# A decode kernel whose first two loads are issued ahead of the opening barrier, and whose closing barrier is taken without GpSimd's drain, with GpSimd waiting for the store

## The chip, the cores and the metric

The kernel runs on one core of one Trainium2 chip. The metric is the time of one execution on the device, in microseconds (us), as the timer gives it. A profile has its own length, the span, from the first to the last instruction that it records; for this kernel the timer reads 1.8 us more than the span. All runs whose times are compared were in the same (fast) state. SP, ACT, DVE, PE and GpSimd (POOL in the profile) are the five engines; SP and ACT issue the loads and stores here.

## The reference, cut to what matters

```python
# x (1,1,640); k_cache, v_cache (1,32,32768,128); wq (640,4096); wo (4096,640)
# w_gate, w_up (640,1728); w_down (1728,640); all bfloat16
xn = layernorm(x)
q  = xn @ wq                                       # 32 heads of 128
p  = softmax(q . k_cache * 128**-0.5)              # one query, 32768 keys for each head
attn = (p . v_cache) @ wo
ffn  = (silu(xn @ w_gate) * (xn @ w_up)) @ w_down
out  = x + attn + ffn                              # 640 numbers
```

Each of the 32 heads has its own K and its own V of 8 MiB. They are read once and used once, so the job is to read 554 MB.

Of the kernel before, what the change touches and what calls it, by code (L numbers as in the profile page):

```python
# [12 lines left out]
def bass_parallel_sum__gqa_block_cached__swiglu_ffn__decode_kernel(  # L13
# [18 lines left out]
    NCD = D // 128  # L32
# [46 lines left out]
    with ExitStack() as es:  # L79
# [3 lines left out]
        def sem(name):  # L83
            return es.enter_context(nc.semaphore(name))
# [32 lines left out]
        s_x, s_wq, s_out = sem("x"), sem("wq"), sem("o")  # L117
# [13 lines left out]
        s_att, s_fin = sem("att"), sem("fin")  # L131
        s_xr, s_or = sem("xr"), sem("orow")
        s_ob, s_op, s_ot = sem("o_blocks"), sem("o_ps"), sem("o_rows")
        block = es.enter_context(nc.Block())

        flat = ring[:, :, :].rearrange("p s n -> p (s n)")
        wq = flat[:, WQ_S * CE:WQ_S * CE + NCD * H * DH]
        x0 = WQ_S * CE + NCD * H * DH
        xrow = flat[0:1, x0 + NCD * 128:x0 + NCD * 128 + D]
        xrow_v = xrow.rearrange("o (m c) -> o m c", c=NCD)  # L140
        xnb = flat[:, x0:x0 + NCD * 128].rearrange("p (c m) -> p c m", c=NCD)
        assert NCD * (H * DH + 256) <= CE
        wq_v = wq.rearrange("p (c n) -> p c n", c=NCD)
        f0 = FFN_S * CE
        wg = flat[:, f0:f0 + NCD * F]
        wu = flat[:, f0 + NCD * F:f0 + 2 * NCD * F]
# [15 lines left out]
        def kv_src(cache, h, j0, n):  # L162
            return cache[0, h].rearrange("(p j) d -> p (j d)", p=128)[:, j0 * DH:(j0 + n) * DH]

        def counter(e, h0):

            group = [None]

            def wait(sem_of, h, count):
                n = count(h)  # L170
                if group[0] is not None:
                    d = count(h + PER) - n
                    assert n >= 1 and all(count(h + PER * i) == n + d * i for i in range((H - h0) // PER))
                    n = group[0] * d + n
                e.wait_ge(sem_of, n)

            return group, wait

        def at(tile, h, n, i):

            start = h * n if i is None else i * (PER * n) + h * n
            return tile[:, bass.ds(start, n)]

        with nc.psum_tensor("ps8", [128, 8, 512], F32) as ps8:
# [10 lines left out]
            @block.sync  # L195
            def sp(e):
                owner = {}
                for u in units:
                    s = slot_of[u]
                    if s in owner:  # L200
                        e.wait_ge(*owner.pop(s))
                    if u[0] == "wq":
                        e.dma_start(wq, A_wq.rearrange("(p c) n -> p (c n)", c=NCD)).then_inc(s_wq, 16)  # L203
                        owner[s] = (s_q, NQB)
                    elif u[0] == "k":
                        e.dma_start(ring[:, s, :], kv_src(A_k_cache, u[1], 0, NJ)).then_inc(s_slot[s], 16)
                        owner[s] = (s_qk, NHF * (u[1] + 1))
                    elif u == LASTV:
                        j = 0
                        for i, n in enumerate(TAIL):  # L210
                            e.dma_start(ring[:, s, j * DH:(j + n) * DH],
                                        kv_src(A_v_cache, u[1], j, n)).then_inc(s_tail[i], 16)
                            j += n
                    elif u[0] == "v":
                        e.dma_start(ring[:, s, :], kv_src(A_v_cache, u[1], 0, NJ)).then_inc(s_slot[s], 16)
                        owner[s] = (s_pv, u[1] + 1)
                    elif u[0] == "ffn":
                        e.dma_start(wg, B_w_gate.rearrange("(p c) n -> p (c n)", c=NCD)).then_inc(s_ffn[0], 16)
                        e.dma_start(wu, B_w_up.rearrange("(p c) n -> p (c n)", c=NCD)).then_inc(s_ffn[1], 16)
                        e.dma_start(flat[:, d0:d0 + FM * D], B_w_down[0:FM * 128, :].rearrange(  # L220
                            "(p j) n -> p (j n)", j=FM)).then_inc(s_ffn[2], 16)
                        e.dma_start(wd[0:FL, FM, :], B_w_down[FM * 128:F, :]).then_inc(s_ffn[2], 16)
                    else:
                        wo_src = A_wo.rearrange("(p j) n -> p (j n)", j=OC)
                        j = 0
                        for i, n in enumerate(WTAIL):
                            e.dma_start(wo[:, j * D:(j + n) * D], wo_src[:, j * D:(j + n) * D]).then_inc(s_wo[i], 16)  # L227
                            j += n
                e.wait_ge(s_fin, 2)
                e.dma_start(out[0, 0:1, :].rearrange("o (c m) -> (o c) m", c=NCD), orow[:, :]).then_inc(s_out, 16)  # L230
                e.wait_ge(s_out, 16)

            @block.gpsimd
            def pool(g):
                n = [0]

                def done(ins):
                    ins.then_inc(s_const, 1)
                    n[0] += 1
                    g.wait_ge(s_const, n[0])  # L240

                for t in (ident, identf):
                    done(g.memset(t[:, :], 0.0))
                    done(g.affine_select(out=t[:, :], in_=t[:, :], compare_op=ALU.not_equal, fill=1.0, base=0,
                                         pattern=[[-1, 128]], channel_multiplier=1))
                done(g.memset(blk[:, :], 0.0))
                for a in range(RB):
                    done(g.tensor_copy(out=fold32[a * 32:(a + 1) * 32, :],
                                       in_=ident[a * 32:(a + 1) * 32, a * 32:a * 32 + OC]))
                for a in range(RB):  # L250
                    done(g.memset(blk[a * 32:(a + 1) * 32, a:a + 1], 1.0))
                assert n[0] == 5 + 2 * RB

            @block.tensor
            def pe(t):
# [172 lines left out]

            @block.scalar
            def act(a):  # L430
                a.dma_start(xrow, A_x[0, 0:1, :]).then_inc(s_x, 16)
                a.sem_inc(s_ov, 1)
                a.wait_ge(s_a, 8)
                a.activation(out=st[:, 4:5], in_=st[:, 3:4], func=ACTF.Sqrt).then_inc(s_aa, 1)
                for b in range(NQB):
                    a.wait_ge(s_q, b + 1)
                    a.activation(out=qb[:, b * 512:(b + 1) * 512], in_=bank[b], func=ACTF.Copy).then_inc(s_qc, 1)

                group, wait = counter(a, HA)

                def evac(h):
                    wait(s_pv, h, lambda h: h + 1)
                    wait(s_rz, h, lambda h: h + 1)
                    if h >= 1 and group[0] is None:
                        a.wait_ge(s_fold, h)
                    a.activation(out=o4[:, :], in_=O, func=ACTF.Copy,  # L446
                                 scale=rzb[0:W, h % SR:h % SR + 1]).then_inc(s_o4, 1)

                def column(h):
                    wait(s_fold, h, lambda h: h + 1)  # L450
                    a.activation(out=at(ocol, h, 1, group[0]), in_=fold_ps, func=ACTF.Copy).then_inc(s_ov, 1)  # L451

                def softmax(h):
                    wait(s_neg, h, lambda h: h + 1)
                    a.activation(out=P[:, h % PR, :], in_=sc[:, :], func=ACTF.Exp,  # L455
                                 bias=negb[:, h % SR:h % SR + 1], scale=c_scale,
                                 accum_out=rsum[:, h % SR:h % SR + 1]).then_inc(s_exp, 1)

                def step(h):
                    if h >= 3:  # L460
                        column(h - 3)
                    if h >= 2:
                        evac(h - 2)
                    softmax(h)

                for h in range(HA):
                    step(h)
                with a.Fori(0, (H - HA) // PER) as i:
                    group[0] = i
                    for h in range(HA, HA + PER):  # L470
                        step(h)
                    group[0] = None
                column(H - 3)
                evac(H - 2)
                column(H - 2)
                a.wait_ge(s_op, 1)
                a.activation(out=ot[:, :], in_=op, func=ACTF.Copy).then_inc(s_ot, 1)
                a.wait_ge(s_f, 1)
                a.activation(out=sg[:, 0, 0:FB - 1], in_=ffn[:, 0:FB - 1], func=ACTF.Exp,
                             scale=-1.0).then_inc(s_fa, 1)  # L480
                a.activation(out=sg[0:FL, 0, FB - 1:FB], in_=ffn[0:FL, FB - 1:FB], func=ACTF.Exp,
                             scale=-1.0).then_inc(s_fa, 1)
# [140 lines left out]
```

## The kernel before: the parts that the change and the argument touch

All large loads go through a ring of three slots in SBUF, and SP issues all of them in order: wq, K0, K1, V0, K2, V1, ... until the last V, the three FFN weights and wo. Before it reuses a slot, SP waits until its last user has read it. ACT issues the one small load, of x (1280 bytes). Each engine's program is a branch of one block; a block ends with a barrier of all engines. The framework puts another barrier in front of it, after GpSimd has set a few constants.

```python
        s_ob, s_op, s_ot = sem("o_blocks"), sem("o_ps"), sem("o_rows")
        block = es.enter_context(nc.Block())       # default closing barrier
        # ... (cut)

            @block.sync
            def sp(e):
                owner = {}
                for u in units:                    # wq, K0, K1, V0, K2, V1, ...
                    s = slot_of[u]
                    if s in owner:
                        e.wait_ge(*owner.pop(s))
                    if u[0] == "wq":
                        e.dma_start(wq, A_wq.rearrange("(p c) n -> p (c n)", c=NCD)).then_inc(s_wq, 16)
                        owner[s] = (s_q, NQB)
                    elif u[0] == "k":
                        e.dma_start(ring[:, s, :], kv_src(A_k_cache, u[1], 0, NJ)).then_inc(s_slot[s], 16)
                        # ... (cut: V, FFN weights, wo)
                e.wait_ge(s_fin, 2)
                e.dma_start(out[0, 0:1, :].rearrange("o (c m) -> (o c) m", c=NCD), orow[:, :]).then_inc(s_out, 16)
                e.wait_ge(s_out, 16)               # the store has landed

            @block.gpsimd
            def pool(g):
                n = [0]

                def done(ins):                     # each constant waits for the one before
                    ins.then_inc(s_const, 1)
                    n[0] += 1
                    g.wait_ge(s_const, n[0])
                # ... (cut: identity matrices and masks)
                for a in range(RB):
                    done(g.memset(blk[a * 32:(a + 1) * 32, a:a + 1], 1.0))
                assert n[0] == 5 + 2 * RB

            @block.scalar
            def act(a):
                a.dma_start(xrow, A_x[0, 0:1, :]).then_inc(s_x, 16)
                # ... (cut)
```

## Time and profile before

| | before |
|---|---|
| time, median of 4 runs (lowest to highest) | 1288.67 us (1288.64 to 1289.19) |
| span of the profile | 1286.8 us |
| moved, rate over the span | 554 MB, 431 GB/s |
| PE, DVE busy | 81%, 52% |
| first packet of wq moves at | 1.79 us |
| issue of the store to the end of the span | 1.58 us |

The page of the kernel before, cut to its DMA lines. The rows DMA and GB/s have one entry for each fortieth of the span; a 9 is 90% or more of the 16 DMA engines busy.

```profile
DMA  9999999999999999999999999999999999999998
GB/s 422 426 424 449 426 430 441 430 434 428 440 428 432 444 428 432 440 430 434 428 440 428 432 444 428 432 440 428 434 428 442 428 432 444 428 432 440 428 418 358
...
q1 hardware_dynamic: 11178, 554.00, 99.7%
```

The loads bound this kernel. They are never starved: the queue of SP was busy for 99.7% of the time of all 16 engines, and only the first and the last of the 40 slices contain a stretch without load. PE and DVE idle for a part of every head, waiting for K or V. The Trainium skill, "DMA: Bandwidth & Descriptors", section "Specifications", gives 435 GB/s as the ceiling of the fabric, and the 431 GB/s of this trace agrees with that.

The timeline of the kernel before, from 0 to 17 us, cut to loads and to what uses them. Columns: start and length in us, engine (SPq and ACTq are the queues that issue), line, operation, written<-read, count, and in brackets how long the engine had been idle and what ended it.

```profile
0.74 0.52 ACTq L431 DMA_DIRECT2D ring<-in_A_x_dram  x1
0.75 0.42 SPq L203 DMA_DIRECT2D ring<-in_A_wq_dram  x1
1.23 0.88 SPq L206 DMA_DIRECT2D ring<-in_A_k_cache_dram  x2
...
2.04 0.35 PE L260 MATMUL ps<-one,ring 1*128 1x1 bf16 x5 [2.04 <-DMA ring<-in_A_x_dram]
...
6.16 0.82 DVE L513 COPY ring<-xn 128x640 bf16<-128x640 bf16 x1
...
16.26 1.01 PE L275 MATMUL ps<-ring 128*128 128x512 bf16 x2 [11.17 <-DMA ring<-in_A_wq_dram]
```

The packets of the same kernel from 0 to 4 us, one entry for each 0.1 us (bytes are counted where a packet starts; the 13 is x, what follows is wq):

```profile
GB/s 0 0 0 0 0 0 0 0 0 0 0 0 0 0 0 0 13 819 1229 3277 410 410 0 0 0 410 0 0 0 0 0 0 0 0 0 0 0 0 0 1229
```

So the layernorm (PE L260 to DVE L513) is done at 6.98 us, and then PE waits until wq lands, for 9.3 us.

The instructions of the opening barrier in the kernel before (the view of one source line, here the framework's). Columns: operation, count, duration in ns (min/median/max), first and last start in us.

```profile
L608 POOLq EVENT_SEMAPHORE  x2: 17/17/17, 0.5 to 0.6; - x2
L608 SPq DRAIN  x1: 7/7/7, 0.0 to 0.0; - x1
...
L608 SPq EVENT_SEMAPHORE  x1: 17/17/17, 0.7 to 0.7; - x1
```

A barrier works like this: each engine drains (by an instruction DRAIN; that of DVE before the closing, for example, ended 0.05 us after the last operation of DVE) and counts itself in; GpSimd waits for the four others (its first EVENT_SEMAPHORE, "gather"), and then lets them go (the second, "release"). SP counted itself in at 0.00 us and stood until 0.66 us, because GpSimd first set its constants. That wait is what the change is after.

The closing barrier before, in the same view:

```profile
L79 POOLq EVENT_SEMAPHORE  x2: 17/17/17, 1286.6 to 1286.7; - x2
...
L79 SPq COMPARE_BRANCH  x1: 33/33/33, 1286.4 to 1286.4; - x1
L79 SPq DRAIN  x1: 7/7/7, 1286.6 to 1286.6; - x1
```

SP's wait for the store rides on its branch to the end of the block. In the records: the store is issued at 1285.186 us, its last packet starts at 1286.037, the branch goes at 1286.388, SP drains at 1286.553, GpSimd gathers at 1286.586 and releases at 1286.664, and PE, the last to leave, ends at 1286.769.

The end of the chain of waits before, from the last large load on (start us, length us, what):

```profile
1253.62 29.08 DMA ring<-in_A_wo_dram
1282.70 0.05 issue
1282.75 1.49 PE ps L402 x40
...
1284.88 0.28 DVE orow L594
```

### The profile page before, as it was taken

What the parts mean: (1) busy time and instruction counts of PE and PEld (TensorE: products, weight loads), DVE (VectorE), ACT (ScalarE), POOL (GpSimd) and SP (SyncE); (2) the same over time, 40 slices, a digit from 0 to 9 for tenths busy, and PEclk for the clock granted to TensorE, in tenths of its full rate; (3) what the DMA queues carried; (4) which work ended last, traced back from release to release, by engine and by line L of the source; (5) the groups of instructions that cost most, each with busy time, mean ns of one, the idle gap of its engine ahead of it and who ended that gap; (6) DMA issues with size and microseconds to landing.
All of it is one profiled execution on the core that took longest, in us unless ns stands there. A gap on an engine that the chain in (4) does not pass through costs nothing.

```text
span 1286.8 us, 9861 instructions
## 1 busy us (share of the span) xinstructions
PE 1044.2 (81%) x5153; PEld 261.3 (20%) x3234; DVE 670.3 (52%) x409; ACT 52.2 (4%) x140; POOL 2.5 (0%) x17
## 2 busy tenths in 40 slices
PE   4599778789777888778798777798777798778797
PEld 1011112221112221112221112221112221112227
DVE  0855665445664446664446664446664446654440
ACT  2000000000000000000000000000000000000000
POOL 0000000000000000000000000000000000000000
PEclk9799888898888998888898888998888998888995
DMA  9999999999999999999999999999999999999998
GB/s 422 426 424 449 426 430 441 430 434 428 440 428 432 444 428 432 440 430 434 428 440 428 432 444 428 432 440 428 434 428 442 428 432 444 428 432 440 428 418 358
DMA packets 11192, 554.17 MB, mean 431 GB/s; under 512 B 1259, under 2 KB 1452, under 8 KB 1708
## 3 DMA queue, kind: packets, MB, share of 16 engines
q1 hardware_dynamic: 11178, 554.00, 99.7%
q8 instruction: 9, 0.15, 0.0%
q14 instruction: 3, 0.02, 0.0%
q10 hardware_dynamic: 2, 0.00, 0.0%
HBM read 553.99 MB, written 0.00 MB: 431 GB/s over the span
## 4 chain that ended last, share of the span: by engine, by line
DMA 53%; PE 30%; DVE 11%; issue 6%; SPq 0%; DVEq 0%
DMA ring<-in_A_k_cache_dram 51%; PE ps L315 17%; PE ps L283 11%; DVE ring L532 10%; DMA ring<-in_A_wo_dram 2%; PE ps L302 1%; PE ps L357 0%; PE ps L351 0%; PE ps L345 0%; PE ps L402 0%; SPq L227 0%; DVEq L532 0%; DVE sc L538 0%; DVE pmax L544 0%; SPq L203 0%
## 5 line engine op out<-in xcount | busy, mean ns | idle before, releaser
L532 DVE TENSOR_TENSOR ring<-ring,qb 128x8192 bf16<-128x8192 bf16 x128 | 557.8, 4420 | 315.6 <-DMA ring<-in_A_k_cache_dram 315.6
L283 PE MATMUL ps<-ring,ident 128*128 128x512 bf16 x1920 | 500.0, 419 | 0.0
L315 PE MATMUL ps<-ring,P 128*4 128x512 bf16 x1984 | 443.3, 379 | 0.0
L302 PE MATMUL ps<-ring,ident 128*128 128x512 bf16 x128 | 55.9, 437 | 217.8 <-DVE ring L532 217.6
L315 PEld LDWEIGHTS ps<-ring,P 128*4 128x4 bf16 x1984 | 163.4, 85 | 237.8
L302 PEld LDWEIGHTS ps<-ring,ident 128*128 128x128 bf16 x128 | 12.6, 99 | 616.9 <-DVE ring L532 343.6
L538 DVE TENSOR_REDUCE sc<-ps 128x64 f32<-128x512 f32 x128 | 82.2, 683 | 63.5 <-PE ps L283 63.5
L550 DVE TENSOR_SCALAR negb<-ps 128x1 f32<-128x1 f32 x32 | 5.1, 158 | 108.4 <-PE ps L357 108.4
L455 ACT ACTIVATE P<-sc,negb 128x256 bf16<-128x256 f32 x32 | 16.2, 507 | 956.5 <-DVE negb L550 956.5
L547 DVE TENSOR_REDUCE m<-ps 1x1 f32<-1x128 f32 x32 | 8.9, 278 | 85.2 <-PE ps L351 85.2
L337 PEld LDWEIGHTS ps<-identf,o 4*128 4x128 f32 x248 | 30.3, 188 | 13.1 <-issue 13.1
L337 PE MATMUL ps<-identf,o 4*128 4x1 f32 x248 | 32.9, 250 | 0.0
L345 PEld LDWEIGHTS ps<-rsum,ones 128*128 128x128 f32 x64 | 12.1, 190 | 99.9 <-issue 99.0
L446 ACT ACTIVATE o<-ps,rzb 4x512 f32<-4x512 f32 x31 | 21.0, 678 | 6.2 <-PE ps L315 6.2
L275 PE MATMUL ps<-ring 128*128 128x512 bf16 x39 | 11.3, 458 | 11.2 <-DMA ring<-in_A_wq_dram 11.2
L451 ACT ACTIVATE ocol<-ps 128x1 f32 (+1 forms) x31 | 5.4, 173 | 222.0 <-PE ps L337 222.0
L544 DVE TENSOR_REDUCE pmax<-sc 128x1 f32<-128x256 f32 x32 | 13.4, 420 | 0.0
L351 PE MATMUL ps<-identf,pmax 128*1 128x128 f32 x64 | 12.2, 273 | 1.2 <-DVE pmax L544 1.2
L357 PE MATMUL ps<-m,ones 1*128 1x1 f32 x64 | 12.1, 256 | 0.4 <-DVE m L547 0.4
L357 PEld LDWEIGHTS ps<-m,ones 1*128 1x128 f32 x64 | 9.4, 182 | 14.2 <-issue 13.5
L381 PE MATMUL ps<-xn,ring 128*128 128x1 bf16 (+1 forms) x140 | 8.9, 198 | 1.0 <-issue 1.0
L520 DVE RECIPROCAL rzb<-ps 128x1 f32<-128x1 f32 x32 | 5.0, 158 | 8.1 <-PE ps L345 8.1
(62 smaller groups left out, 81.1 us busy)
## 6 DMA issues: line engine op xcount, KB each, us to landing
ring<-in_A_wq_dram SPq DMA_DIRECT2D x1, 5120.0 KB, 15.4
ring<-in_A_v_cache_dram SPq DMA_DIRECT2D x1, 4096.0 KB, 31.8
ring<-in_A_wo_dram SPq DMA_DIRECT2D x3, 1280.0 KB, 25.0
ring<-in_B_w_gate_dram SPq DMA_DIRECT2D x1, 2160.0 KB, 23.0
ring<-in_B_w_up_dram SPq DMA_DIRECT2D x1, 2160.0 KB, 27.7
ring<-in_B_w_down_dram SPq DMA_DIRECT2D x1, 2080.0 KB, 31.8
ring<-in_A_v_cache_dram SPq DMA_DIRECT2D x1, 2048.0 KB, 36.4
ring<-in_A_v_cache_dram SPq DMA_DIRECT2D x2, 1024.0 KB, 39.4
```

The source lines that it names most:

```text
L283: return t.add_instruction(mybir.InstMatmult(start_tensor_calc=False, stop_tensor_calc=stop, tile_size=(128, 128), tile_position=(0, 0), l ...
L302: t.matmul(ob, lhsT=ident[:, :], rhs=src, start=True, stop=False)
L315: mm = t.matmul(O, lhsT=P[:, h % PR, j:j + W], rhs=ring[:, s, j * DH:(j + W) * DH], start=(j == 0), stop=(j + W == NJ))
L337: mm = t.matmul(fold_ps, lhsT=o4[:, m * DH:(m + 1) * DH], rhs=identf[0:W, m:m + 1], start=(m == 0), stop=(m == W - 1))
L345: t.matmul(misc[:, 129:130], lhsT=ones[:, :], rhs=rsum[:, h % SR:h % SR + 1], start=True, stop=True).then_inc(s_z, 1)
L351: t.matmul(misc[0:1, 0:128], lhsT=pmax[:, h % SR:h % SR + 1], rhs=identf[:, :], start=True, stop=True).then_inc(s_t, 1)
L357: t.matmul(misc[:, 128:129], lhsT=ones[0:1, :], rhs=m1[0:1, h % SR:h % SR + 1], start=True, stop=True).then_inc(s_b, 1)
L446: a.activation(out=o4[:, :], in_=O, func=ACTF.Copy, scale=rzb[0:W, h % SR:h % SR + 1]).then_inc(s_o4, 1)
L455: a.activation(out=P[:, h % PR, :], in_=sc[:, :], func=ACTF.Exp, bias=negb[:, h % SR:h % SR + 1], scale=c_scale, accum_out=rsum[:, h % SR: ...
L532: v.tensor_tensor(out=kh, in0=kh, in1=q[:, None, :].to_broadcast([128, HF, DH]), op=ALU.mult).then_inc(s_mul, 1)
L538: v.tensor_reduce(out=sc[:, i * HF:(i + 1) * HF], in_=bank[i].rearrange("p (j e) -> p j e", e=G), axis=AX.X, op=ALU.add).then_inc(s_red, 1)
L544: v.tensor_reduce(out=pmax[:, h % SR:h % SR + 1], in_=sc[:, :], axis=AX.X, op=ALU.max).then_inc(s_max, 1)
```

## The change

The intent: the loads of wq and of x depend on nothing that the opening barrier guards, so they can start before it. The function `ahead` emits a load and then moves it in front of the issuing engine's DRAIN in the first block. At the end, the closing barrier is taken without GpSimd's drain, and GpSimd, which is the barrier's hub, waits for the store in SP's place. The argument `no_gpsimd_drain=True` takes away GpSimd's drain. This is what "semaphore-only barrier" stands for below.

```diff
-        block = es.enter_context(nc.Block())
...
+        def ahead(start):
+            at_start = nc.main_func.blocks[0]
+            n = len(at_start.instructions)
+            start()
+            ins = list(at_start.instructions)
+            new = ins[n:]
+            drain = next(i for i, x in enumerate(ins)
+                         if x.engine == new[0].engine and type(x).__name__ == "InstDrain")
+            at_start.instructions = ins[:drain] + new + ins[drain:n]
+
+        ahead(lambda: nc.sync.dma_start(wq, A_wq.rearrange("(p c) n -> p (c n)", c=NCD)).then_inc(s_wq, 16))
+        ahead(lambda: nc.scalar.dma_start(xrow, A_x[0, 0:1, :]).then_inc(s_x, 16))
+        block = es.enter_context(nc.Block(no_gpsimd_drain=True))
...
                     if u[0] == "wq":
-                        e.dma_start(wq, A_wq.rearrange("(p c) n -> p (c n)", c=NCD)).then_inc(s_wq, 16)
                         owner[s] = (s_q, NQB)
...
-                e.wait_ge(s_out, 16)                  # SP
...
+                g.wait_ge(s_out, 16)                  # GpSimd, its last line
...
-                a.dma_start(xrow, A_x[0, 0:1, :]).then_inc(s_x, 16)
```

## The prediction

> **What bounds the kernel now.** The loads do. On the page the DMA row is 9 in 39 of 40 slices, the load queue's packets took 99.7% of 16 engines' time, and 554 MB moved at 431 GB/s over the span of 1286.8 us. PE is busy 81%, DVE 52%. The Trainium skill, "DMA: Bandwidth & Descriptors", Specifications, gives a fabric ceiling of 435 GB/s; this trace agrees. By the packets' own times nearly all 16 engines work from 2.1 us to 1281.8 us without a hole, and K and V loads land a median of 41.4 and 36.7 us after issue. So the stream never starves in the middle, and three things could shorten the run: an earlier first packet, fewer bytes, or a shorter tail behind the last packet. The change touches the first and the end of the third.
>
> **Start.** Timeline of the first microsecond: SP reaches the opening barrier at 0.00 us (DRAIN of 7 ns), ACT at 0.13, PE at 0.32; GpSimd sets constants and drains until 0.50, gathers at 0.54, releases at 0.62; SP issues the wq load at 0.75 (0.42 us long). The first wq packet moves at 1.79, 1.04 us after the issue began. Ahead of the barrier the issue begins at about 0.00, so the first packet should move at about 1.04: 0.75 us earlier. SP then drains at about 0.42, before GpSimd gathers. ACT's x issue (0.52 us) moves from 0.74 to about 0.13 and ends about 0.65, so ACT arrives last and the barrier opens 0.1 to 0.2 us later. Nothing critical sees that: the K load starts at about 1.0 instead of 1.23, behind 5 MB of wq; the layernorm ends at 7.0 us and waits until wq lands at 16.2. The stream is contiguous, so all of the 0.75 us should reach the end.
>
> **End.** The store is issued at 1285.19, its last packet moves at 1286.04, SP branches on the semaphore at 1286.39 and drains at 1286.55; GpSimd gathers at 1286.59, releases at 1286.66; the others leave at 1286.71 and the span ends at 1286.77. With GpSimd waiting, its own arrival is the last: the SP-to-GpSimd hop (0.03 us) goes, perhaps more. The drains removed on ACT, PE, DVE and GpSimd (0.04 to 0.32 us) ended long before, and are worth nothing. Estimate: 0.03 to 0.1 us.
>
> **Sum.** 0.75 + 0.05 = 0.8 us of 1288.67, 0.06%. Predicted 1287.9 us, 8 times in 10 between 1287.0 and 1288.8. The three runs before spread over 0.52 us. Faster by over 2%: 0.5%; within: 99%; slower: 0.5%.
>
> **What would show it.** First wq packet at about 1.0 us instead of 1.8; first matmul 0.5 to 0.6 us earlier; first q matmul at about 15.5 instead of 16.26; the chain of waits still DMA, then PE; store issue at about 1284.4; from the store's issue to the span's end 1.50 to 1.55 us instead of 1.58.
>
> **What would make it wrong.** If SP's DRAIN waits for the load in flight, not only its issue, the barrier opens after 15 us, K is issued late and the stream gets a hole of about 1 us: the gain is eaten. If the queue is not ready at 0.00, less is gained. If the span itself begins earlier by the moved issue, the timer may show nothing. If GpSimd wakes slower than SP on the store's semaphore, the end gains nothing.

## The result, and the profile after

| | before | after |
|---|---|---|
| time, median of 4 runs (lowest to highest) | 1288.67 us (1288.64 to 1289.19) | 1288.01 us (1287.94 to 1288.06) |
| span of the profile | 1286.8 us | 1286.3 us |
| first packet of wq moves at | 1.793 us | 1.024 us |
| the opening barrier releases at | 0.622 us | 0.926 us |
| issue of the store | 1285.186 us | 1284.633 us |
| issue of the store to the end of the span | 1.583 us | 1.626 us |

The ratio is 0.9994, with a 95% interval of 0.9977 to 1.0011. Ratios are the mean time of one kernel's fast runs over that of the other's in the same rounds, so not quite the ratio of the medians. That interval is wider than the effect. What makes the gain believable is that the runs don't overlap: the kernel before ran 31 times, between 1288.57 and 1289.20 us, and the changed kernel 9 times, between 1287.81 and 1288.25.

The DMA lines of the page after: the same rate and the same share, so the stream ran as before but for its start.

```profile
DMA  9999999999999999999999999999999999999998
GB/s 424 424 450 427 429 438 431 430 430 444 428 432 442 428 432 434 436 428 432 442 430 432 436 432 430 430 444 428 432 442 428 432 432 438 428 432 442 430 417 355
...
q1 hardware_dynamic: 11178, 554.00, 99.7%
```

The timeline after, from 0 to 17 us, the same lines of it:

```profile
0.00 0.41 SPq L154 DMA_DIRECT2D ring<-in_A_wq_dram  x1
0.12 0.51 ACTq L155 DMA_DIRECT2D ring<-in_A_x_dram  x1
...
1.05 1.25 SPq L218 DMA_DIRECT2D ring<-in_A_k_cache_dram  x2
...
1.54 0.27 PEld L272 LDWEIGHTS ps<-one,ring 1*128 1x128 bf16 x5 [1.54 <-DMA ring<-in_A_x_dram]
...
5.66 0.82 DVE L524 COPY ring<-xn 128x640 bf16<-128x640 bf16 x1
...
15.47 1.86 PE L287 MATMUL ps<-ring 128*128 128x512 bf16 x4 [10.88 <-DMA ring<-in_A_wq_dram]
```

Its packets from 0 to 4 us, as above (in the trace x starts at 1.01 us and wq at 1.02 us):

```profile
GB/s 0 0 0 0 0 0 0 0 0 0 2470 2048 410 0 410 410 0 0 410 410 0 0 0 0 0 0 0 0 0 0 0 0 1638 819 1638 819 819 0 410 0
```

The wq load is now the first instruction of the program, 0.75 us earlier, and the q projection starts 0.79 us earlier. The opening barrier after:

```profile
L619 POOLq EVENT_SEMAPHORE  x2: 17/17/17, 0.8 to 0.9; - x2
...
L619 SPq DRAIN  x1: 117/117/117, 0.5 to 0.5; - x1
L619 ACTq DRAIN  x1: 137/137/137, 0.7 to 0.7; - x1
```

The drains that took 7 and 8 ns on SP and ACT took 117 and 137 ns behind an issue, and ACT, whose issue takes longer and starts later, is the last to arrive; the barrier opens 0.30 us later than before. The K loads are issued behind it, and still 0.17 us earlier than before, since SP has no wq left to issue.

The closing after (from the views of lines L79 and L264):

```profile
L79 SPq DRAIN  x1: 152/152/152, 1285.1 to 1285.1; - x1
L79 POOLq COMPARE_BRANCH  x1: 33/33/33, 1285.9 to 1285.9; - x1
...
L264 POOLq EVENT_SEMAPHORE  x1: 17/17/17, 1285.8 to 1285.8; - x1
```

GpSimd's wait for the store (L264) has become an instruction of its own in front of the branch. Step by step, from the records, in us:

| step | before (SP waits) | after (GpSimd waits) |
|---|---|---|
| issue of the store to its last packet | 0.851 | 0.851 |
| last packet to the end of the wait | 0.351 (on the branch) | 0.361 (own instruction) |
| that instruction to the branch | none | 0.066 |
| branch to GpSimd's gather | 0.198 (through SP's drain) | 0.162 |
| gather to release | 0.078 | 0.080 |
| release to the last engine's end | 0.105 | 0.106 |
| sum | 1.583 | 1.626 |

And the end of the chain of waits after, 0.5 to 0.6 us earlier than before but otherwise the same. That is less than the 0.77 us of the start because the stretch from the first packet to the store was 0.22 us longer in this trace; in that of `after_again`, the same kernel, it was 0.03 us shorter than before. One pair of traces can't show how much of the start reaches the end; the series of runs below has to:

```profile
1253.07 29.08 DMA ring<-in_A_wo_dram
1282.15 0.05 issue
1282.19 1.49 PE ps L414 x40
...
1284.33 0.28 DVE orow L605
```

### The profile page after: what moved, and what is told of

Read it like the earlier page. It is cut to its first block, busy times and chain, and to the rows that moved or that the text cites. A ratio compares the mean times of both kernels' runs of the same rounds, so it can differ in the third digit from the quotient of the medians.

```text
span 1286.3 us, 9864 instructions
## 1 busy us (share of the span) xinstructions
PE 1041.6 (81%) x5153; PEld 261.4 (20%) x3234; DVE 670.4 (52%) x409; ACT 52.2 (4%) x140; POOL 2.5 (0%) x17
## 4 chain that ended last, share of the span: by engine, by line
DMA 53%; PE 30%; DVE 11%; issue 6%; DVEq 0%; SPq 0%
DMA ring<-in_A_k_cache_dram 51%; PE ps L327 17%; PE ps L295 11%; DVE ring L543 10%; DMA ring<-in_A_wo_dram 2%; PE ps L314 1%; PE ps L369 0%; PE ps L363 0%; PE ps L357 0%; PE ps L414 0%; SPq L239 0%; DVEq L543 0%; DVE sc L549 0%; DVE pmax L555 0%; DVEq L188 0%
```

## The experiments

The theory after the result (A): all of the gain is the earlier first packet of wq, because the stream of loads has no slack; the new closing costs 0.04 us and hides in the noise. The rivals: the closing gains as predicted (B); the stream has slack, so that the gain came from elsewhere (C); the x load carries a part of it (D). Where the text below gives a difference from before, it is the difference of the means.

### The halves, and the start moved the other way

`start_only` has both loads ahead and the closing as before; `close_only` is the reverse; `after_again` is the changed kernel again. `late_wq` is the kernel before with one line more:

```diff
                     if u[0] == "wq":
+                        e.wait_ge(s_x, 16)
                         e.dma_start(wq, A_wq.rearrange("(p c) n -> p (c n)", c=NCD)).then_inc(s_wq, 16)
```

> Both loads ahead of the opening barrier, the closing as before (SP waits for the store, default closing barrier). Theory A (all the gain is the earlier first packet, the new closing costs 0.04 us): time 0.70 to 0.80 us below the kernel before and 0 to 0.1 us below the changed kernel; first wq packet at 1.02 us, from store issue to end of span 1.58 us. Theory B (the closing is worth 0.05 us as predicted): 0.05 us above the changed kernel, and less than 0.65 below before.

> The loads as before, only the closing changed. Theory A: from store issue to end of span 1.62 to 1.63 us against 1.58, so time equal to before or up to 0.05 us above it; first wq packet at 1.79 us as before. Theory B: 1.50 to 1.55 us, time 0.03 to 0.1 us below before.

> The changed kernel once more, on this chip, to have it in the same rounds as its parts. Both theories: 0.6 to 0.8 us below before; store issue to end 1.63 us again if that was no chance of one trace.

> The kernel before, with SP waiting for the landing of x before it issues wq: the start shifted the other way. From the trace of before x lands about 2.0 us, so wq is issued at about 2.05 instead of 0.75 and its first packet should move at about 3.1 instead of 1.79: 1.3 us later. Theory A (the stream has no slack, a delay of its first packet is paid in full): 1.2 to 1.4 us above before. Rival C (the stream has slack in later waits on the ring, and the measured 0.66 us came from elsewhere): less than 0.5 us above before.

| kernel | median of 5 (lowest to highest) | mean, minus that of before | store issue to end |
|---|---|---|---|
| before (9 runs) | 1288.84 (1288.69 to 1289.07) | | |
| start_only | 1288.11 (1287.96 to 1288.39) | -0.67 | 1.582 |
| close_only | 1288.83 (1288.76 to 1288.99) | 0.00 | 1.619 |
| after_again | 1287.99 (1287.81 to 1288.25) | -0.81 | 1.621 |
| late_wq | 1290.10 (1290.00 to 1290.23) | +1.26 | 1.587 |

The change of the closing alone gains nothing on the timer, and its stretch in the trace is 0.04 us longer, twice. Rival B falls. Against the expectation, `start_only` was slower than the changed kernel by 0.14 us of mean, which by the timer alone would have spoken for B. The runs of the two overlap, their starts are the same code, and `wq_ahead` below, with the same closing as `start_only`, came out 0.76 us below before; so this is taken as noise: the timer can't show 0.04 us here, and the stretch in the trace has to. `late_wq` moved the first packet of wq from 1.79 to 3.03 us, here in its trace from 0 to 4 us, and cost just that: rival C falls.

```profile
GB/s 0 0 0 0 0 0 0 0 0 0 0 0 0 0 0 0 13 0 0 0 0 0 0 0 0 0 0 0 0 0 2458 2048 0 819 0 819 0 0 0 0
```

### One load at a time

In `wq_ahead` and `x_ahead` the closing is as before, and only one of the two calls of `ahead` is kept; the other load is issued where it was.

```diff
 # wq_ahead, against start_only (x_ahead: the other way round)
         ahead(lambda: nc.sync.dma_start(wq, ...).then_inc(s_wq, 16))
-        ahead(lambda: nc.scalar.dma_start(xrow, A_x[0, 0:1, :]).then_inc(s_x, 16))
...
             def act(a):
+                a.dma_start(xrow, A_x[0, 0:1, :]).then_inc(s_x, 16)
```

> Only the wq load ahead of the opening barrier; x is issued behind it, the closing is as before. Theory A (only the first wq packet counts): first wq packet at 1.02 us, barrier opens at about 0.70 us, x lands about as late as in the kernel before, layernorm done at about 7 us, far ahead of wq; time 0.65 to 0.80 us below before, as with both loads ahead. Rival D (the x load carries part of the gain): 0.2 us or more above the version with both ahead, so only 0.3 to 0.5 us below before.

> Only the x load ahead; wq is issued behind the barrier. Theory A: ACT's issue and the drain after it hold the barrier until about 0.93 us instead of 0.62, so wq is issued at about 1.05 instead of 0.75 and its first packet moves at about 2.1 instead of 1.79; time 0.25 to 0.35 us ABOVE before. Rival D: x earlier helps, time at or below before.

`wq_ahead` ran at 1288.11 us (1287.83 to 1288.21), 0.76 below before; `x_ahead` at 1289.06 (1288.94 to 1289.48), 0.30 above it. Rival D falls: x gives nothing by itself, and moved alone it even costs, because ACT's issue and drain hold the barrier (released at 0.935 us) behind which wq now waits. Put together, the kernels with five rounds that keep a wait for the store in front of the closing barrier line up on the first packet of wq, whose time is from the records of one trace each (`fused` is described in the next section):

| kernel | first wq packet, us | minus before (1.793) | mean time, minus that of before |
|---|---|---|---|
| start_only | 1.027 | -0.77 | -0.67 |
| after_again | 1.027 | -0.77 | -0.81 |
| fused | 1.028 | -0.77 | -0.79 |
| wq_ahead | 1.049 | -0.74 | -0.76 |
| close_only | 1.771 | -0.02 | 0.00 |
| x_ahead | 2.111 | +0.32 | +0.30 |
| late_wq | 3.031 | +1.24 | +1.26 |

One us at the start is one us at the end, within 0.1 us, in both directions.

One part of what was expected of `wq_ahead` was wrong, and is the more useful result. Its timeline from 0 to 17 us:

```profile
0.00 0.42 SPq L154 DMA_DIRECT2D ring<-in_A_wq_dram  x1
...
0.81 0.51 ACTq L442 DMA_DIRECT2D ring<-in_A_x_dram  x1
...
7.07 0.35 PE L271 MATMUL ps<-one,ring 1*128 1x1 bf16 x5 [7.07 <-DMA ring<-in_A_x_dram]
...
11.19 0.82 DVE L524 COPY ring<-xn 128x640 bf16<-128x640 bf16 x1
...
15.32 2.29 PE L286 MATMUL ps<-ring 128*128 128x512 bf16 x5 [5.20 <-DMA ring<-in_A_wq_dram]
```

x was issued at 0.81 us, about as in the kernel before, but behind wq, and its first packet moved only at 5.13 us, after 4.3 us, instead of 0.91 us after its issue. The layernorm was done at 12.0 us and had 3.3 us left of its 9.3. The Trainium skill, "DMA: Bandwidth & Descriptors", section "Queues, rings and completion order", says that each DMA engine serves its queues in turn, a whole packet at a time. The trace agrees in part. The records don't name the engine, but after the first on each engine nearly every packet starts 3 or 4 ns before another one ends, which is taken to be the one ahead of it on its engine. So x can be placed: its engine moved packets of wq (40960 bytes each) at 1.05 us (2.57 us long) and 3.62 us (1.51 us long), then x at 5.13 us, another wq packet at 5.19 us (1.51 us long), and x's semaphore write of 4 bytes at 6.70 us. So x's data and its semaphore write took turns with whole packets of wq. But by an estimate from the other traces, where the first packet of x moved 0.90 to 0.94 us after its issue, x was ready at about 1.7 us, and still two packets of wq went by, not one. Why, stays open; no run shows whether the page means by a packet what the profile counts as one.

With both ahead, x's first packet moved at 1.01 to 1.04 us in seven of nine traces, but at 1.43 us in that of `wait_last_pe` and at 1.78 us in that of `start_only`. No packet of wq can have held it up there: in these nine traces the first one to end did so at 3.15 us or later. What did is not known. So in these traces, moving x too kept the layernorm from being pushed toward the critical path; it is insurance, not gain.

### The closing, taken apart

`fused` is the changed kernel without GpSimd's own wait for its last constant (the users of that constant have their own). `start_sem_sp` and `start_drain_pool` have one half of the new closing each, over the new start. The last two have one run each, and are read from their traces only.

```diff
 # fused, against the changed kernel
                 for a in range(RB):
-                    done(g.memset(blk[a * 32:(a + 1) * 32, a:a + 1], 1.0))
+                    ins = g.memset(blk[a * 32:(a + 1) * 32, a:a + 1], 1.0)
+                    if a < RB - 1:
+                        done(ins)
+                    else:
+                        ins.then_inc(s_const, 1)
+                        n[0] += 1
 # start_sem_sp, against start_only (SP waits for the store)
-        block = es.enter_context(nc.Block())
+        block = es.enter_context(nc.Block(no_gpsimd_drain=True))
 # start_drain_pool, against the changed kernel (GpSimd waits)
-        block = es.enter_context(nc.Block(no_gpsimd_drain=True))
+        block = es.enter_context(nc.Block())
```

> The changed kernel without GpSimd's own last wait for its last constant (others still wait for that constant), so that its wait for the store can ride on its branch. Theory E (the closing costs 0.04 us because two waits in front of one branch need an instruction of their own, 0.066 us): from store issue to end of span 1.555 to 1.565 us against 1.62. Rival F (GpSimd sees the semaphore later than SP, or the semaphore-only barrier is slower): 1.60 us or more. The time itself: within 0.15 us of the changed kernel, too little to show.

> Both loads ahead, the semaphore-only closing barrier, but SP waits for the store as before (one wait, which rides on its branch). Separates the two halves of the new closing; the measure is the stretch from store issue to end of span, which repeated to 0.006 us. Theory E (the whole cost is GpSimd's second wait): 1.58 us or less. Rival F2 (the semaphore-only barrier costs as much or more, since each engine now drains and then arrives with an instruction of its own): 1.60 to 1.64 us.

> Both loads ahead, GpSimd waits for the store, but the closing barrier is the default one with GpSimd's drain. Theory E: 0.066 us for the second wait, less the hop from SP, plus GpSimd's own drain (0.04 us before) now that it comes after the store: 1.64 to 1.68 us from store issue to end of span, so the semaphore-only barrier is worth 0.02 to 0.05 us once GpSimd waits. Rival F2: no more than the changed kernel's 1.62.

Issue of the store to the end of the span, us:

| | default closing barrier | semaphore-only barrier |
|---|---|---|
| SP waits for the store | 1.583 (before), 1.582 (start_only), 1.587 to 1.589 (late_wq, wq_ahead, x_ahead) | 1.663 (start_sem_sp) |
| GpSimd waits, two waits before its branch | 1.693 (start_drain_pool) | 1.626, 1.621, 1.619 (after, after_again, close_only) |
| GpSimd waits, one wait before its branch | not run | 1.559 (fused) |

Theory E held for `fused`: with one wait, it rides on the branch, and the 0.066 us go. The lines of its trace (line L79):

```profile
L79 SPq DRAIN  x1: 152/152/152, 1285.1 to 1285.1; - x1
L79 POOLq COMPARE_BRANCH  x1: 33/33/33, 1285.9 to 1285.9; - x1
```

There is no wait of GpSimd's at another line any more. For the other two E was wrong as it stood: `start_sem_sp` lost more than even the rival expected, and `start_drain_pool` lost in the direction that E gave, 0.013 us beyond its range. Each half of the new closing costs by itself: the semaphore-only barrier with SP waiting 0.08 us, since SP's count-in is then an instruction of its own behind its drain (drain to count-in 0.063 us, count-in to gather 0.042; before, drain to gather 0.033); GpSimd as the waiter with the default barrier 0.11 us: 0.066 us for the second wait's instruction, and most of the rest because GpSimd's own drain now comes after the store (branch to gather 0.233 us, against 0.198 before through SP's drain). Together they cost 0.04. The semaphore-only barrier is worth 0.07 us once GpSimd waits, and nothing else in this closing gains. The timer shows none of this: `fused` ran at 1288.05 us (1287.88 to 1288.19).

### A wait behind the barrier

If the branch, the gather, the release and the leaving are 0.41 us in series behind the store, they can run while the store is in flight, with the wait for it as the last instruction of the program:

```diff
 # wait_last, against the changed kernel
+        es.callback(lambda: nc.sync.wait_ge(s_out, 16))    # runs when the block has been closed
         block = es.enter_context(nc.Block(no_gpsimd_drain=True))
...
-                g.wait_ge(s_out, 16)
 # wait_last_pe: nc.tensor in the place of nc.sync
```

> The changed kernel with the wait for the store moved behind the closing barrier, on SP, as the last instruction of the program: the barrier runs while the store is in flight. From the traces the store's last packet moves 0.85 us after its issue, the wait ends 0.36 us later. Theory G (the branch, gather, release and leaving after the store are a serial 0.41 us that can be hidden): store issue to end 1.22 to 1.24 us against 1.62, time 0.35 to 0.45 us below the changed kernel, 1.1 to 1.2 below before. Rival: the wait costs as much there, or the time on the timer doesn't follow the span: less than 0.2 us below the changed kernel.

> The version with SP's wait behind the closing barrier once more, beside the next one. Store issue to end of span 1.22 us again; time 1.2 to 1.5 us below before; timer less span 1.45 us again against 1.82 for all others.

> The same with TensorE instead of SP as the engine that waits behind the barrier. The timer less the span fell from 1.82 to 1.45 us with SP waiting last. Theory H1 (what each engine does after its last instruction takes longer on some than on SP, and with SP last the others do it during the store): span as with SP, but timer less span back near 1.8, time 0.3 to 0.4 us above the SP version. Theory H2 (any single engine that ends last is enough, the rest is common): 1.45 us again and the same time as the SP version.

| kernel | median of 5 (lowest to highest) | mean, minus that of before | store issue to end | timer less span, mean |
|---|---|---|---|---|
| after_again | 1287.99 (1287.81 to 1288.25) | -0.81 | 1.621 | 1.84 |
| wait_last | 1287.36 (1287.30 to 1287.74) | -1.37 | 1.223 | 1.45 |
| wait_last_again (another chip) | 1287.32 (1287.17 to 1287.45) | -1.50 | 1.222 | 1.49 |
| wait_last_pe (another chip) | 1287.70 (1287.48 to 1288.05) | -1.09 | 1.266 | 1.68 |

The lines of the second of these runs: the barrier is through at 1285.4 us, and SP's wait at L156 is the last instruction.

```profile
L79 POOLq EVENT_SEMAPHORE  x2: 17/17/17, 1285.2 to 1285.3; - x2
L79 SPq DRAIN  x1: 152/152/152, 1285.0 to 1285.0; - x1
...
L156 SPq EVENT_SEMAPHORE  x1: 17/17/17, 1285.8 to 1285.8; - x1
```

Theory G held: the stretch is 0.40 us shorter. The time fell further than expected, since the timer also reads less beyond the span, 1.45 and 1.49 us instead of 1.8. These two parts make 0.75 to 0.79 us, of which the means show 0.56 and 0.69 below `after_again`; the rest is of the size by which the stretch before the store scatters. This version beats both kernels, in all of its 10 runs (1287.17 to 1287.74 against 1287.81 to 1288.25 of the 9 of the changed kernel), though by 0.05% only. Five of the 10 are from another chip, on which the kernel before had nearly the same median as on the first (1288.82 us, against 1288.77 and 1288.84). It still waits for the store before the program ends.

What the timer counts after the span can't be seen in a trace. `wait_last_pe` was to tell whether it depends on which engine ends last. It came out between the two theories: 1.68 us, with a time 0.41 us above that of SP (0.19 us of it beyond the span, 0.04 us the longer stretch, and the rest a longer time up to the store, which scatters as said). The direction is that of H1, the size is not. That the ending engine matters is shown; how, stays open.

## Why the prediction was right or wrong

The time was right: 1287.9 us predicted, 1288.01 measured, inside the range; and so was the main reason.

- **"So the stream never starves in the middle" and "all of the 0.75 us should reach the end".** Right. The first packet moved 0.77 us earlier, the mean time fell by 0.79 and 0.81 us in the two calls. Shifted by +0.32 and +1.24 us, the stream carried +0.30 and +1.26 to the end.
- **SP's drain waits for the issue only.** Right: it took 117 ns, not the 15 us that wq needs to land.
- **"The barrier opens 0.1 to 0.2 us later".** Its size was off: 0.30 us, since a drain behind an issue took 117 to 137 ns where the trace before showed 7 and 8. Off the critical path with both loads ahead, as predicted; `x_ahead` shows what it costs when wq stands behind it.
- **"First matmul 0.5 to 0.6 us earlier".** Roughly right in the two traces of the changed kernel (weights for it loaded at 1.54 us instead of 2.04), but not dependable: in `start_only` it came at 2.4 us, since x's first packet moved only at 1.78 us, for a reason that the trace doesn't show. The prediction had not thought of x and wq as sharing engines; `wq_ahead` shows the size of that, 4.3 us from issue to first packet instead of 0.9.
- **"Store issue at about 1284.4".** 1284.63 us in the trace of the result and 1284.39 in that of `after_again`: the stretch before the store scatters by this much, so the second is no proof and the first no failure.
- **"With GpSimd waiting, its own arrival is the last: the SP-to-GpSimd hop (0.03 us) goes, perhaps more. Estimate: 0.03 to 0.1 us."** This step failed, in sign. The hop did go (branch to gather 0.162 instead of 0.198 us), but GpSimd's branch already had a wait on it, for its last constant, so the wait for the store needed an instruction of its own, 0.066 us, and was seen 0.010 us later. The sum is a loss of 0.04 us. Without that second wait (`fused`) the closing gains 0.02 us, still less than the estimate.
- **"The drains removed on ACT, PE, DVE and GpSimd ... are worth nothing".** The premise was wrong: only GpSimd's drain is removed; the four others keep theirs and count themselves in with one more instruction each. With SP waiting that costs 0.08 us (`start_sem_sp`); with GpSimd waiting, it is off the path.
- **The sum.** The failed step was 0.05 us of 0.8 in the prediction, too little to move the time out of its range. That the fall of the means, 0.79 and 0.81 us, meets the predicted 0.80 so closely is luck: the parts as measured in the traces make 0.77 - 0.04 = 0.73 us, and the medians of the result differ by 0.66.

## What to carry to other kernels

Where a stream of loads is never starved, as here, its first packet is on the critical path, and a load that depends on nothing belongs ahead of the opening barrier. In this kernel that paid one us for one us; but look at which small load then falls in line behind the large one, and move that as well. Only one engine has to wait for the last store: that wait can stand behind the closing barrier, so that the barrier runs while the store is in flight. A change of such a size is judged by a short stretch inside the trace, if it repeats from trace to trace, or by a series of shifts of the same thing, and not by the timer alone.

## What the Trainium skill lacked or had wrong

- "DMA: Bandwidth & Descriptors", section "Bandwidth", "Where 436 GB/s comes from": it says that between HBM and SBUF the limit of about 358 GB/s for one core binds. That doesn't hold for this program, which runs on one core and read 431 GB/s over its whole span. A note of the same section keeps the 358 to the case of both cores streaming, and has 425 GB/s for a single core; the sentence should say so too.
- The same page, "Specifications": it gives a first-byte latency of about 0.6 us for loads issued by SP or ACT, but not from where this is counted. With nothing ahead of them, the first packet moved 0.61 to 0.63 us after the end of SP's issue of wq (128 rows of 40960 bytes), which agrees, and 1.02 to 1.05 us after its beginning; for x on ACT it was 0.38 to 0.43 us after the end and 0.90 to 0.94 us after the beginning.
- "VectorE: DVE Perf Modes", section "The DRAIN you can't avoid": it names two kinds of DRAIN, the flush after each DVE operation and the runtime's own of a constant 12 ns or so. The drains in the barriers of this program are in neither: they took 7 to 10 ns on an idle engine, but 117 to 153 ns right behind the issue of a load or a store on SP, 132 to 138 ns on ACT, and 257 to 323 ns on ACT, PE and DVE where the engine's last work was still running.
- "Perfetto Trace Analysis", section "Identifying Dependency Chains": it says that an instruction with several waits may get an extra semaphore instruction in front of it, but not what that costs. With two waits in front of one branch it was 0.066 us from the extra instruction to the branch, on GpSimd.
- No page has it: the time on the timer beyond the span depends on which engine ends last, 1.8 us with all leaving the barrier together, 1.45 to 1.49 with SP alone last, 1.68 with PE alone last.
